# Attention's values products in float32, even and odd key tiles in two halves of the array's columns

## The chip, the cores and the metric

One core of a Trainium2 chip runs the whole program. TensorE (PE, with its weight loads as PEld) multiplies into PSUM; VectorE (DVE), ScalarE (ACT) and GpSimd (POOL) do the rest, and SyncE's queue (SP) issues the transfers. The metric is the device time of one execution in microseconds; a kernel is timed by the median of its runs.

## What is computed

Three layers follow each other. The first is attention with a mask: each query and key is assigned to the nearest of 16 centroids, and a query sees only the keys of its own cluster. Batch 2, 8 heads, 768 tokens, 64 numbers a head. The two layers behind it (a token and channel mixer, and one with cosine and sine) are not touched by the change.

```python
scores = scale * np.matmul(q, k.transpose(0, 1, 3, 2))
scores = np.where(mask, scores, -1000000000.0)
scores = scores - np.max(scores, axis=-1, keepdims=True)
attn = np.exp(scores)
attn = attn / (np.sum(attn, axis=-1, keepdims=True) + 1e-09)
return np.matmul(attn, v).astype(np.float32)
```

## The kernel before

Products are made near float32 accuracy out of a rounded format, float32r, which the array takes in one trip: an operand x is split into h = round(x) and l = x - h, and the products of the parts are summed in PSUM. A split costs one rounding copy and one subtraction (`split_sb`, `split_ps`).

The attention stage goes through 48 units in order. A unit is 256 queries (two tiles of 128) of one head; a head has three units, a pair of heads six, and there are eight pairs. With n for the loop's turn, PE gets `scores(n)`, `turn(n-1)` and `values(n-2)` (`SKEW = 2`), and a scheduler puts the instructions of each engine in their final order: one that stands later in the program can come earlier if it is ready.

- `scores` (line 381): for each of two query tiles four products of 384 columns into a PSUM tile of two banks (two such tiles), DVE's negated maximum over 768 columns (`nm`, line 401), ACT's exponential into `e` (line 403).
- `turn` (line 410): the numerators `e` are turned so that keys lie in partitions, three PSUM tiles `t` of 512 columns (two key tiles by 256 queries), four turns each (line 418). Each tile is then split into `ph` and `pl`, in float32r. By `KINDS` two of three tiles are of kind A: ACT rounds `ph` out of PSUM and DVE subtracts `pl` (lines 87, 88). The third is of kind C: ACT copies the tile to `raw` (line 424), POOL makes `ph` and `pl` from it (lines 428, 429). The first two units and the last are all of kind A.
- `values` (line 435): the values v are split once a head by POOL into `vs`, with v's rounded part in columns 0 to 63 and its rest in columns 64 to 127 (`load_v`, line 325). Per unit twelve products of 128 stationary columns and 256 moving ones (line 444): six key tiles, each with `ph` and `pl`. Rows 0 to 63 of the result hold the part of the rounded values, rows 64 to 127 that of the rests. ACT copies the lower half to `tmp`, DVE adds the two halves into `xt` (lines 449, 451). There is one PSUM bank for the result.
- `natural` (line 455): once a pair, six turns of `xt` back, and DVE scales by the sums of the numerators.
- `masks` (line 234), once a pair, for the next pair: four float32 products of 32 stationary columns at four places in the array's columns (`sim`, line 244), then DVE's transposition, maximum, comparison `eq` (line 257), second transposition, a counting product `pp` on PE (line 268) and the one-hot rows.
- `split_pair` (line 341), once a pair, on POOL: the split of the next pair's queries and keys. `tok_x` (line 130) splits the tokens of the next layer on POOL, six times behind units 29 to 39 and, there, behind the last raw split (`marks["raw"]`). `load_w` prepares weights of the next layers.

Of the kernel before, what the change touches and what calls it, by code (L numbers as in the profile page):

```python
# [9 lines left out]
F32 = mybir.dt.float32  # L10
F32R = mybir.dt.float32r
BF16 = mybir.dt.bfloat16
U32 = mybir.dt.uint32
AF = mybir.ActivationFunctionType
ALU = mybir.AluOpType
# [3 lines left out]
P = 128  # L19
# [4 lines left out]
C2 = 2.0 * math.pi - 6.28125  # L24
PI_LO = 3.1415925


KINDS = "AACAACAAC"
RAW = 4
HL = 4  # L30

X_AT = (29, 31, 33, 35, 37, 39)
# [10 lines left out]
SKEW = 2  # L43
# [4 lines left out]
def tile_model(ctx: ExitStack, tc: tile.TileContext, qT, kT, v, cent, w1, w2, wc1, wc2, wth, wri, wch, out):  # L48


    nc = tc.nc
    B, H, D, S = qT.shape
    NT = S // P
# [12 lines left out]
    marks = {}  # L66
# [8 lines left out]
    def split_sb(h, l, x, rnd, sub):  # L75

        if rnd == "p":
            nc.gpsimd.tensor_scalar(out=h, in0=x, scalar1=1.0, scalar2=0.0, op0=ALU.mult, op1=ALU.add)
        elif rnd == "v":
            nc.vector.tensor_copy(out=h, in_=x)  # L80
        else:
            marks["h"] = nc.scalar.activation(out=h, in_=x, func=AF.Copy)
        e = nc.gpsimd if sub == "p" else nc.vector
        return e.tensor_tensor(out=l, in0=x, in1=h.bitcast(F32), op=ALU.subtract)

    def split_ps(h, l, ps):
        a = nc.scalar.activation(out=h, in_=ps, func=AF.Copy)  # L87
        return a, nc.vector.tensor_tensor(out=l, in0=ps, in1=h.bitcast(F32), op=ALU.subtract)  # L88
# [41 lines left out]
    def tok_x(b, s, new, by):  # L130

        h, l = (new(f"x{k}{b}{s}") for k in "hl")
        marks["l"] = split_sb(h, l, xn[b * NT + s], *by)
        xs.setdefault(b, []).append((h, l))
# [24 lines left out]
    with ExitStack() as actx:  # L159
        ap = actx.enter_context(tc.tile_pool(name="attn", bufs=1))  # L160
# [39 lines left out]
        for j in range(2):  # L200
            r = slice(64 * j, 64 * j + 64)
# [121 lines left out]
        pairs = {}  # L323

        def load_v(b, h):
            vr = ap.tile([P, NT * D], F32, tag="vr", bufs=2, name=f"vr{b}{h}")
            nc.sync.dma_start(out=vr, in_=v[b, h])
            vs = ap.tile([P, NT, 2 * D], F32R, tag="vs", bufs=2, name=f"vs{b}{h}")
            v3 = vr.rearrange("p (n d) -> p n d", d=D)
            split_sb(vs[:, :, 0:D], vs[:, :, D : 2 * D], v3, "p", "p")  # L330
            return vs

        def load_pair(b, pr):
            ts = []
# [75 lines left out]
        def turn(b, h, u, es):  # L410

            pr = []
            for j in range(NT // 2):
                ps = ps_t.tile([P, 2, 256], F32, tag="t", name=f"t{b}{h}{u}{j}")
                for i in range(2):
                    for a in range(2):
                        kt = 2 * j + a
                        marks["turn"] = nc.tensor.transpose(ps[:, a, i * P : i * P + P], es[i][:, kt * P : kt * P + P], ident)  # L418
                ph = ap.tile([P, 2, 256], F32R, tag="ph", bufs=6, name=f"ph{b}{h}{u}{j}")
                pl = ap.tile([P, 2, 256], F32R, tag="pl", bufs=6, name=f"pl{b}{h}{u}{j}")  # L420
                kind = "A" if (b, h, u) in (units[0], units[1], units[-1]) else KINDS[3 * u + j]
                if kind in "BC":
                    raw = ap.tile([P, 2, 256], F32, tag="pr", bufs=2, name=f"pr{b}{h}{u}{j}")
                    nc.scalar.activation(out=raw, in_=ps, func=AF.Copy)  # L424
                    if kind == "B":
                        nc.scalar.activation(out=ph, in_=ps, func=AF.Copy)
                    else:
                        nc.gpsimd.tensor_scalar(out=ph, in0=raw, **one)  # L428
                    marks["raw"] = nc.gpsimd.tensor_tensor(out=pl, in0=raw, in1=ph.bitcast(F32), op=ALU.subtract)  # L429
                else:  # L430
                    marks["ph"], marks["pl"] = split_ps(ph, pl, ps)
                pr.append((ph, pl))
            return pr

        def values(b, h, u, pr, vs):

            if (b, h, u) == units[-1]:
                ps = ps_s.tile([P, 2, 512], F32, tag="s", name="olast")[:, 0, :]
            else:
                ps = ps_o.tile([P, 512], F32, tag="o", name=f"o{b}{h}{u}")  # L440
            order = range(NT)
            for n, kt in enumerate(order):
                for k, p in enumerate(pr[kt // 2]):
                    nc.tensor.matmul(  # L444
                        ps[:, :256], vs[:, kt, :], p[:, kt % 2, :],
                        start=n == 0 and k == 0, stop=n == NT - 1 and k == 1,
                    )
            tmp = ap.tile([64, 256], F32, tag="tmp", bufs=2, name=f"tmp{b}{h}{u}")
            marks["tmp"] = nc.scalar.activation(out=tmp, in_=ps[64:128, :256], func=AF.Copy)
            r0 = 64 * (h % 2)  # L450
            nc.vector.tensor_tensor(  # L451
                out=xts[b, h // 2][r0 : r0 + 64, u * 256 : u * 256 + 256], in0=ps[0:64, :256], in1=tmp, op=ALU.add
            )

        def natural(b, pr):

# [28 lines left out]
        gen = iter(())  # L485
        units = [(b, h, u) for b, h in heads for u in range(NT // 2)]
        es, prs = {}, {}
        late = []
        for n in range(len(units) + SKEW):
            if n < len(units):  # L490
                b, h, u = units[n]
                if u == 0 and h % 2 == 0:
                    sums[b, h // 2] = small.tile([P, NT, 2], F32, tag="sm", bufs=2, name=f"sm{b}{h}")
                    xts[b, h // 2] = ap.tile([P, S], F32, tag="xt", bufs=2, name=f"xt{b}{h}")
                if n != 1:
                    es[n] = scores(b, h, u, ops[b, h])
                if n == 0:
                    next(first, None)
                    place(1, ms[0, 0])
                    scored = marks["scores"]  # L500
                    es[1] = scores(*units[1], ops[b, h])
                    with tc.issue_after(marks["max"].ins):
                        ops[heads[1]] = prep_first(*heads[1])
                    marks["scores"] = scored
                    for w, k in zip(WARM[1:], ("cps", "sim", "scores")):
                        with tc.issue_after(marks[k].ins):
                            warm_up(w)
                h1 = n // 3 + 1
                if 1 < h1 < len(heads) and u == PREP[h1 % 2]:
                    b2, h2 = heads[h1]  # L510
                    ops[b2, h2] = prep(b2, h2, ms[b2, h2 // 2])
                p1 = n // 6 + 1
                if p1 < len(heads) // 2:
                    pr = heads[2 * p1][0], heads[2 * p1][1] // 2
                    if n % 6 == PAIR_AT[0]:
                        raws = load_pair(*pr)
                    if n % 6 == PAIR_AT[1]:
                        split_pair(*pr, raws)
                    if n % 6 == PAIR_AT[2]:
                        gen = masks(*pr)  # L520
            if n >= 3:
                for _ in range(PACE):
                    next(gen, None)
            if n == 42:
                mctx.close()
            if 0 <= n - 1 < len(units):
                prs[n - 1] = turn(*units[n - 1], es.pop(n - 1))
            if n < 3:
                with tc.issue_after((marks["turn"] if n else marks["scores"]).ins):
                    for _ in range(PACE):  # L530
                        next(gen, None)
            if 0 <= n - SKEW:
                b, h, u = units[n - SKEW]
                values(b, h, u, prs.pop(n - SKEW), ops[b, h][4])
                if h % 2 == 1 and u == NT // 2 - 1:
                    late.append((n + 1, b, h // 2))
            while late and (n >= late[0][0] or n == len(units) + SKEW - 1):
                _, b, pr = late.pop(0)
                natural(b, pr)
            if n in X_AT:  # L540
                with tc.issue_after(marks["raw"].ins):
                    tok_x(0, X_AT.index(n), part, "pp")
            if n in W1_AT:
                with tc.issue_after(marks["exp"].ins):
                    i = len(w1s)
                    w1s.append(load_w(w1[:, i * 512 : i * 512 + 512], f"w1_{i}", W1_AT[n]))
            if n == len(units):
                with tc.issue_after(marks["tmp"].ins), tc.issue_after(marks["ph"].ins), tc.issue_after(marks["pl"].ins):
                    for i in range(NT // 2):
                        w2s.append(load_w(w2[:, :, i * 256 : i * 256 + 256], f"w2_{i}", "pv"))  # L550

# [252 lines left out]
```

## Time and profile before

| | us |
|---|---|
| median of 3 runs | 685.1 (683.76 to 690.17) |
| the profiled execution | 684.49 |
| its span | 682.8 |
| busy PE, PEld, DVE, ACT, POOL | 649.9, 553.9, 437.0, 367.4, 367.2 |
| mean granted TensorE clock | 0.987 of full speed |

The span is the profiled part of one execution. A busy PE is not a PE at its peak: matmuls are pipelined and their ends are modelled, so the time that a matmul holds the array is read from one start to the next. The chain of waits follows the work that ended last backwards; its PE pieces run from start to start. A group's line gives the count, the busy time, the mean of one in ns, and the engine's idle time ahead of it with what ended it. PEclk 1.0 is 2.4 GHz, 0.5 is 1.2 GHz.

### The profile page before, as it was taken

To read this page: it belongs to the slowest core of one execution; us is meant where nothing else is said; L and a number is where in the kernel's file an instruction comes from. 1 tells how busy PE (TensorE), PEld (TensorE's weight loads), DVE (VectorE), ACT (ScalarE), POOL (GpSimd) and SP (SyncE) were. 2 spreads that over 40 slices of the span, in tenths; PEclk is the share of its full clock that TensorE was granted. 3 is DMA by queue.
4 is the path that set the end of the run, shared out by engine and by line. 5 is a ranking of instruction groups with operands and counts; after the bars stand their busy time and mean duration, and the time that the engine had idled before them with its cause. 6 is when DMAs were issued, how large, how long until landed. Compare 5 with 4: busy or idle time off the path is not lost.

```text
span 682.8 us, 10123 instructions
## 1 busy us (share of the span) xinstructions
PE 649.9 (95%) x3591; PEld 553.9 (81%) x3591; DVE 437.0 (64%) x700; ACT 367.4 (54%) x701; POOL 367.2 (54%) x353
## 2 busy tenths in 40 slices
PE   7899999989979998999999999999999999999997
PEld 5788897988869786888888878888887878888886
DVE  5988989898897985657665434446668784422112
ACT  6687887877857883336543530327578683320000
POOL 8285957759786853116886630512458787532000
PEclk9999999999989999999999999999999999999999
DMA  8554745445451312002443420220021424310001
GB/s 289 160 137 102 176 108 142 110 118 117 94 120 46 86 55 94 32 31 94 143 135 125 139 77 31 63 62 0 1 63 61 124 64 137 81 59 32 15 32 46
DMA packets 24209, 61.43 MB, mean 90 GB/s; under 512 B 4256, under 2 KB 7520, under 8 KB 24160
## 3 DMA queue, kind: packets, MB, share of 16 engines
q1 hardware_dynamic: 24160, 60.80, 31.4%
q8 instruction: 28, 0.46, 0.3%
q14 instruction: 21, 0.17, 0.1%
HBM read 39.65 MB, written 3.15 MB: 63 GB/s over the span
## 4 chain that ended last, share of the span: by engine, by line
PE 79%; ACT 8%; DVE 6%; issue 3%; POOL 2%; DMA 2%; ACTq 0%; POOLq 0%; DVEq 0%
PE o L444 8%; PE t L418 8%; PE c L125 5%; PE c L126 5%; PE c L124 5%; PE r L124 5%; PE r L126 4%; PE r L125 4%; PE s L398 4%; PE y L126 4%; PE y L125 4%; PE y L124 4%; PE s L399 4%; ACT e L403 2%; ACT ph L87 2%
## 5 line engine op out<-in xcount | busy, mean ns | idle before, releaser
L401 DVE TENSOR_REDUCE nm<-s 128x1 f32<-128x768 f32 x96 | 90.7, 951 | 19.2 <-PE s L399 18.7
L403 ACT ACTIVATE e<-s,nm 128x768 f32<-128x768 f32 x96 | 86.9, 906 | 22.6 <-DVE nm L401 21.3
L418 PE MATMUL t<-ident,e 128*128 128x128 f32 x576 | 80.5, 277 | 5.7 <-DVE pl L88 4.7
L398 PE MATMUL s<-k,qh 128*128 128x384 f32 x188 | 70.3, 374 | 10.4 <-ACT e L403 10.4
L418 PEld LDWEIGHTS t<-ident,e 128*128 128x128 f32 x576 | 66.6, 141 | 14.9 <-DVE pl L88 7.1
L444 PE MATMUL o<-ph,vs 128*128 128x256 f32 x282 | 74.1, 295 | 2.3 <-DVE xt L451 1.9
L444 PE MATMUL o<-pl,vs 128*128 128x256 f32 x282 | 71.7, 287 | 0.0
L88 DVE TENSOR_TENSOR pl<-t,ph 128x512 fp32r<-128x512 f32 x99 | 65.0, 675 | 3.3 <-ACT ph L87 2.1
L399 PE MATMUL s<-k,q 128*128 128x384 f32 x192 | 65.4, 344 | 1.3 <-ACT k L274 1.3
L87 ACT ACTIVATE ph<-t 128x512 fp32r<-128x512 f32 x99 | 55.6, 597 | 14.3 <-PE t L418 10.1
L429 POOL TENSOR_TENSOR pl<-pr,ph 128x512 fp32r<-128x512 f32 x45 | 58.9, 1309 | 1.6
L428 POOL TENSOR_SCALAR ph<-pr 128x512 fp32r<-128x512 f32 x45 | 28.3, 628 | 55.7 <-ACT pr L424 49.7
L444 PEld LDWEIGHTS o<-ph,vs 128*128 128x128 f32 x282 | 54.4, 193 | 4.0 <-DVE xt L451 3.2
L124 PE MATMUL r<-ul,c_h 128*128 128x512 f32 x144 | 56.5, 396 | 0.4 <-DVE ul L88 0.4
L126 PE MATMUL y<-zh,k_h 128*128 128x512 f32 x144 | 56.8, 394 | 0.0
L125 PE MATMUL y<-zh,k_l 128*128 128x512 f32 x144 | 56.8, 394 | 0.0
L125 PE MATMUL c<-c_h,rl 128*128 128x512 f32 x144 | 56.0, 390 | 0.7 <-DVE rl L645 0.7
L124 PE MATMUL y<-zl,k_h 128*128 128x512 f32 x144 | 56.7, 394 | 0.0
L114 POOL TENSOR_TENSOR c_f<-c_f,c_raw 128x512 uint32<-128x512 uint32 x24 | 31.6, 1316 | 45.7 <-issue 28.0
L125 PE MATMUL r<-uh,c_l 128*128 128x512 f32 x144 | 56.1, 390 | 0.0
L126 PE MATMUL r<-uh,c_h 128*128 128x512 f32 x144 | 56.0, 390 | 0.0
L126 PE MATMUL c<-c_h,rh 128*128 128x512 f32 x144 | 56.0, 390 | 0.0
(201 smaller groups left out, 1607.7 us busy)
## 6 DMA issues: line engine op xcount, KB each, us to landing
c_raw<-wc SPq DMA_DIRECT2D x24, 512.0 KB, 3.3
k_raw<-wri SPq DMA_DIRECT2D x18, 512.0 KB, 3.6
qh<-qh SPq DMA_DIRECT2D x28, 192.0 KB, 3.0
k<-kh SPq DMA_DIRECT2D x28, 192.0 KB, 4.0
ql<-qT SPq DMA_DIRECT2D x8, 384.0 KB, 3.1
kl<-kT SPq DMA_DIRECT2D x8, 384.0 KB, 3.8
vr<-v SPq DMA_DIRECT2D x16, 192.0 KB, 2.6
w_raw<-w SPq DMA_DIRECT2D x6, 512.0 KB, 3.9
```

Source lines behind the costliest of these rows:

```text
L87: a = nc.scalar.activation(out=h, in_=ps, func=AF.Copy)
L88: return a, nc.vector.tensor_tensor(out=l, in0=ps, in1=h.bitcast(F32), op=ALU.subtract)
L124: nc.tensor.matmul(ps, ah, bl, start=first and i == 0, stop=False)
L125: nc.tensor.matmul(ps, al, bh, start=False, stop=False)
L126: nc.tensor.matmul(ps, ah, bh, start=False, stop=last and i == n - 1)
L398: nc.tensor.matmul(ps[:, half, :NH], qh[:, c], k1[:, n], start=True, stop=False)
L399: marks["scores"] = nc.tensor.matmul(ps[:, half, :NH], ql[:, c], kk[:, n], start=False, stop=True)
L401: marks["max"] = nc.vector.tensor_reduce(out=nm, in_=ps[:, :, :NH], axis=AX.XY, op=ALU.max, negate=True)
L403: marks["exp"] = nc.scalar.activation(out=e.rearrange("p (a n) -> p a n", a=2), in_=ps[:, :, :NH], func=AF.Exp, bias=nm, accum_out=sums[b, ...
L418: marks["turn"] = nc.tensor.transpose(ps[:, a, i * P : i * P + P], es[i][:, kt * P : kt * P + P], ident)
L429: marks["raw"] = nc.gpsimd.tensor_tensor(out=pl, in0=raw, in1=ph.bitcast(F32), op=ALU.subtract)
L444: nc.tensor.matmul(ps[:, :256], vs[:, kt, :], p[:, kt % 2, :], start=n == 0 and k == 0, stop=n == NT - 1 and k == 1,)
```

## The change

`load_v` loads v as it is, in float32, into three buffers `vs`; POOL's split of v is gone, and `vr`. `turn` copies each of the three tiles `t` once, in float32, into `p` (twelve buffers): the first two by ACT, the third by DVE; the splits into `ph` and `pl` and the raw copies are gone. `values` makes six float32 products a unit: 64 stationary columns, 256 moving ones. Even key tiles go to columns 0 to 63 of the array and rows 0 to 63 of the result, odd ones to columns 64 to 127 and rows 64 to 127; `tmp` and the sum of the two halves stay as they are. `values` may start on PE only behind the last turn that was issued (`issue_after(marks["turn"])`); `GROUP = 1` makes a group of one unit. The first token splits no longer stand behind a raw split, and the last weight loads stand behind `pA` and `pV`.

```diff
-KINDS = "AACAACAAC"
+KINDS = "AAV"
+GROUP = 1
+PB = 12
         def load_v(b, h):
-            vr = ap.tile([P, NT * D], F32, tag="vr", bufs=2, name=f"vr{b}{h}")
-            nc.sync.dma_start(out=vr, in_=v[b, h])
-            vs = ap.tile([P, NT, 2 * D], F32R, tag="vs", bufs=2, name=f"vs{b}{h}")
-            v3 = vr.rearrange("p (n d) -> p n d", d=D)
-            split_sb(vs[:, :, 0:D], vs[:, :, D : 2 * D], v3, "p", "p")
-            return vs
+            vs = ap.tile([P, NT * D], F32, tag="vs", bufs=3, name=f"vs{b}{h}")
+            nc.sync.dma_start(out=vs, in_=v[b, h])
+            return vs.rearrange("p (n d) -> p n d", d=D)
...
-                ph = ap.tile([P, 2, 256], F32R, tag="ph", bufs=6, name=f"ph{b}{h}{u}{j}")
-                pl = ap.tile([P, 2, 256], F32R, tag="pl", bufs=6, name=f"pl{b}{h}{u}{j}")
...
-                    marks["ph"], marks["pl"] = split_ps(ph, pl, ps)
-                pr.append((ph, pl))
+                p = ap.tile([P, 2, 256], F32, tag="p", bufs=PB, name=f"p{b}{h}{u}{j}")
+                if KINDS[j] == "A":
+                    marks["pA"] = nc.scalar.activation(out=p, in_=ps, func=AF.Copy)
+                else:
+                    marks["pV"] = nc.vector.tensor_copy(out=p, in_=ps)
+                pr.append(p)
...
-            for n, kt in enumerate(order):
-                for k, p in enumerate(pr[kt // 2]):
+            for i, (n, pr, vs) in enumerate(us):
+                po = ps[:, 256 * i : 256 * i + 256]
+                for kt in range(NT):
+                    r = 64 * (kt % 2)
                     nc.tensor.matmul(
-                        ps[:, :256], vs[:, kt, :], p[:, kt % 2, :],
-                        start=n == 0 and k == 0, stop=n == NT - 1 and k == 1,
+                        po[r : r + 64, :], vs[:, kt, :], pr[kt // 2][:, kt % 2, :], start=kt < 2, stop=kt >= NT - 2,
+                        tile_position=(0, r),
                     )
...
-                values(b, h, u, prs.pop(n - SKEW), ops[b, h][4])
+                group.append((n - SKEW, prs.pop(n - SKEW), ops[b, h][4]))
+                if len(group) == GROUP:
+                    with tc.issue_after(marks["turn"].ins):
+                        values(group)
+                    group = []
...
             if n in X_AT:
-                with tc.issue_after(marks["raw"].ins):
-                    tok_x(0, X_AT.index(n), part, "pp")
+                tok_x(0, X_AT.index(n), part, "pp")
...
-                with tc.issue_after(marks["tmp"].ins), tc.issue_after(marks["ph"].ins), tc.issue_after(marks["pl"].ins):
+                with tc.issue_after(marks["tmp"].ins), tc.issue_after(marks["pA"].ins), tc.issue_after(marks["pV"].ins):
```

## Rows read from the trace of the kernel before

**Rows 1.** The page: the span, and the chain that ended last by engine.

```profile
span 682.8 us, 10123 instructions
...
PE 79%; ACT 8%; DVE 6%; issue 3%; POOL 2%; DMA 2%; ACTq 0%; POOLq 0%; DVEq 0%
```

**Rows 2.** Windows: stretch, its length, busy us of PE, PEld, DVE, ACT, POOL; clock.

```profile
48.00:78.00 30.00, 28.01 (x210) 25.78 (x209) 26.29 (x46) 23.40 (x50) 21.56 (x23) 1.00 0.52 122
...
195.00:225.00 30.00, 25.09 (x169) 23.52 (x167) 25.80 (x38) 19.25 (x41) 19.34 (x20) 0.89 0.39 88
```

**Rows 3.** The chain of waits, 62 to 105 us: start, length, engine, tile, line.

```profile
62.09 1.44 PE o L444 x12
...
64.23 1.31 PE t L418 x12
...
65.54 0.18 PE s L398
...
69.68 1.07 PE o L444 x9
...
71.46 0.35 PE o L444 x3
...
75.60 0.78 PE sim L244 x8
...
85.30 1.00 ACT e L403 x2
...
104.66 0.78 PE sim L244 x8
```

**Rows 4.** Tile eq (duration min/median/max), then the timeline around 195 us.

```profile
L257 DVE TENSOR_TENSOR eq<-sT,mx x8: 534/1304/4924, 9.5 to 195.0; 128x384 bf16<-128x384 f32 x8
...
195.00 4.92 DVE L257 TENSOR_TENSOR eq<-sT,mx 128x384 bf16<-128x384 f32 x1
...
198.90 0.62 POOL L428 TENSOR_SCALAR ph<-pr 128x512 fp32r<-128x512 f32 x1
...
201.45 1.11 PE L418 MATMUL t<-ident,e 128*128 128x128 f32 x4 [3.55 <-DVE pl L88]
```

**Rows 5.** Timeline around two sim products: start, length, engine, line, tiles, shapes.

```profile
45.07 0.52 PE L244 MATMUL sim<-ql,cst 128*32 128x384 f32 x2
...
45.42 0.49 PE L244 MATMUL sim<-ql,cst 128*32 128x384 f32 x2
...
45.85 0.44 PE L398 MATMUL s<-k,qh 128*128 128x384 f32 x1
...
46.13 0.34 PE L399 MATMUL s<-k,q 128*128 128x384 f32 x1
...
192.56 0.34 PE L399 MATMUL s<-k,q 128*128 128x384 f32 x1
...
192.82 0.52 PE L244 MATMUL sim<-ql,cst 128*32 128x384 f32 x2
...
192.82 0.11 PEld L244 LDWEIGHTS sim<-ql,cst 128*32 128x32 f32 x2 [0.25 <-issue]
...
192.85 0.12 PEld L244 LDWEIGHTS sim<-ql,cst 128*32 128x32 f32 x2
```

**Rows 6.** Groups, 17 to 262 us: shapes, count, busy us, mean ns, idle before.

```profile
L88 DVE TENSOR_TENSOR pl<-t,ph 128x512 fp32r<-128x512 f32 x99 | 65.0, 675 | 3.3 <-ACT ph L87 2.1 <-PE o L444 0.4
...
L87 ACT ACTIVATE ph<-t 128x512 fp32r<-128x512 f32 x99 | 55.6, 597 | 14.3 <-PE t L418 10.1 <-PE o L444 3.5
...
L424 ACT ACTIVATE pr<-t 128x512 f32<-128x512 f32 x45 | 27.1, 603 | 6.7 <-PE t L418 6.4 <-POOL kl L84 0.2
...
L428 POOL TENSOR_SCALAR ph<-pr 128x512 fp32r<-128x512 f32 x45 | 28.3, 628 | 55.7 <-ACT pr L424 49.7 <-PE o L444 5.9
...
L429 POOL TENSOR_TENSOR pl<-pr,ph 128x512 fp32r<-128x512 f32 x45 | 58.9, 1309 | 1.6
...
L250 DVE STREAM_TRANSPOSE sT<-sim 128x384 f32<-128x384 f32 x7 | 4.0, 573 | 0.1
```

More of the change, by code (lines that the diff above doesn't have):

```diff
@@ L418, in turn @@
                         marks["turn"] = nc.tensor.transpose(ps[:, a, i * P : i * P + P], es[i][:, kt * P : kt * P + P], ident)
-                ph = ap.tile([P, 2, 256], F32R, tag="ph", bufs=6, name=f"ph{b}{h}{u}{j}")
-                pl = ap.tile([P, 2, 256], F32R, tag="pl", bufs=6, name=f"pl{b}{h}{u}{j}")
[L421 to L429, printed above, removed]
-                else:
-                    marks["ph"], marks["pl"] = split_ps(ph, pl, ps)
@@ L432, in turn, with values @@
-                pr.append((ph, pl))
-            return pr
-        def values(b, h, u, pr, vs):
-            if (b, h, u) == units[-1]:
+                p = ap.tile([P, 2, 256], F32, tag="p", bufs=PB, name=f"p{b}{h}{u}{j}")
+                if KINDS[j] == "A":
+                    marks["pA"] = nc.scalar.activation(out=p, in_=ps, func=AF.Copy)
+                else:
+                    marks["pV"] = nc.vector.tensor_copy(out=p, in_=ps)
+                pr.append(p)
+            return pr
+        def values(us):
+            if us[-1][0] == len(units) - 1:
@@ L438, in values @@
                 ps = ps_s.tile([P, 2, 512], F32, tag="s", name="olast")[:, 0, :]
             else:
-                ps = ps_o.tile([P, 512], F32, tag="o", name=f"o{b}{h}{u}")
-            order = range(NT)
-            for n, kt in enumerate(order):
-                for k, p in enumerate(pr[kt // 2]):
+                ps = ps_o.tile([P, 512], F32, tag="o", name=f"o{us[0][0]}")
+            outs = []
+            for i, (n, pr, vs) in enumerate(us):
+                po = ps[:, 256 * i : 256 * i + 256]
+                for kt in range(NT):
+                    r = 64 * (kt % 2)
@@ L444, in values @@
                     nc.tensor.matmul(
-                        ps[:, :256], vs[:, kt, :], p[:, kt % 2, :],
-                        start=n == 0 and k == 0, stop=n == NT - 1 and k == 1,
-                    )
[L448 to L453, printed above, removed]
+                        po[r : r + 64, :], vs[:, kt, :], pr[kt // 2][:, kt % 2, :], start=kt < 2, stop=kt >= NT - 2,
@@ new lines, in values @@
+                        tile_position=(0, r),
+                    )
+                outs.append((units[n], po))
+            for (b, h, u), po in outs:
+                tmp = ap.tile([64, 256], F32, tag="tmp", bufs=2, name=f"tmp{b}{h}{u}")
+                marks["tmp"] = nc.scalar.activation(out=tmp, in_=po[64:128, :], func=AF.Copy)
+                r0 = 64 * (h % 2)
+                nc.vector.tensor_tensor(
+                    out=xts[b, h // 2][r0 : r0 + 64, u * 256 : u * 256 + 256], in0=po[0:64, :], in1=tmp, op=ALU.add
+                )
@@ L487, in tile_model @@
         es, prs = {}, {}
-        late = []
+        late, group = [], []
         for n in range(len(units) + SKEW):
```

## Prediction, before the change was run

> **What bounds the kernel now.** I read the page first [rows 1]: 682.8 us of span, and PE is 79% of the chain that ended last. That share is a mean over stages, so I went on to the one stage that the change touches: attention, from the first turned tile at 17 us to about 256. In its windows [rows 2] DVE is busy 26.3 of 30 us and PE 28.0, by modelled ends. The chain of waits [rows 3] tells more, since its PE pieces run from start to start. One unit (256 queries of a head) takes 1.44 for twelve values products, 1.31 for twelve turns and 8 x 0.175 = 1.40 for scores: 4.15 us. A pair of heads is six units, 24.9, and has one cluster product (sim, 0.78), one count product (384 columns, as a score: 0.17) and six turns of its output (6 x 0.109): 26.5 us of PE work. Sim starts at 75.60 and again at 104.66. So a cycle is 29.06 us and PE idles 2.6 of it. The idle is not spread: up to sim the chain is PE alone, after it the chain goes through ACT's exponentials [rows 3]. In that part DVE makes the next pair's masks.
>
> Over the stage: 48 x 4.15 + 8 x 1.6, less 1.7 for the last values products, which run behind it, = 210 of 239 us. About 30 us of PE idle is all that a lighter DVE, ACT or POOL can give back. The rest is PE work.
>
> One piece of it stands out [rows 4]. The mask comparison eq (line 257) takes 0.53 us at its shortest, 1.3 in the middle and 4.92 once. That one ends at 199.92, 0.4 us after a POOL instruction that began at 198.90 and took 0.62: eq reads two SBUF tiles and waits for a gap in POOL. The Trainium skill has such a rule (SBUF — State Buffer, section "Who interferes with whom"): a DVE instruction with two SBUF inputs contends with a GpSimd one that reads SBUF, and the later one blocks. By that rule whatever stays on POOL can still hold eq, and this case would then keep some of its 7 us. Behind eq stand the reduction, the exponential and the turn: PE waits 3.55 us [rows 4], and the mean granted clock from 195 to 225 is 0.89 [rows 2], which is 0.11 x 2 x 30 = 6.6 us at 1.2 GHz. I price the event at 3.55 of waiting and 3.3 lost to half clock, 7 us.
>
> **The change, part by part.** *Values on PE.* Removed: 1.44 us a unit. Added: six float32 products, each with 64 stationary columns, even key tiles in array columns 0 to 63, odd ones in 64 to 127. The nearest rows are sim's [rows 5]: four float32 products side by side, 32 stationary columns and 384 moving ones, two records each. The first records start at 45.07, the second ones at 45.42. So the parts of the array do run together, and a record holds its part for 0.33 to 0.35 us: 384 columns twice at 2.4 GHz (0.32) and a little. For 256 columns that is 0.215 to 0.235. A half has three products, six records, in a row: 1.29 to 1.41. Then the way in and out. In: from 192.56 to 192.82, where a score alone takes 0.175: 0.09. Out: from 45.42 to 45.85 is 0.43, less the record's 0.33: 0.10; and the next product starts 0.28 after that one instead of 0.175: 0.10. Together 0.29 a visit. Values then cost 1.58 to 1.70 a unit; I take 1.61, near the low end, because sim as a whole (0.78 with its way out) fits it. 48 x (1.61 - 1.44) = +8 us, bounds +7 and +12.
>
> *More visits.* In a cycle, some units' twelve products are cut into 9 and 3 [rows 3], two of the six. That costs nothing today; after the change each piece is a visit of its own. Values are now placed behind the last turn, which forbids a cut by turns, but not one by scores. Two cuts in eight cycles are 16 extra visits at 0.29: 0 to +5, I take +2.
>
> *Evacuations* [rows 6]. Removed, over the three tiles of a unit: ACT's ph, DVE's pl (675 ns), ACT's raw copy, POOL's ph and pl (628 and 1309 ns). Added: two ACT copies and one DVE copy a unit. ACT's price is that of its raw copy, 603 ns. A DVE copy of 512 columns out of PSUM has no row; below by DVE's 384-column transposition out of PSUM (573), above by L88 (675), which reads the same tile and another. I take 0.65, by L88. DVE: 99 x 0.675 - 48 x 0.65 = 36 us less in the stage, some 4.2 a cycle. ACT: 99 x 0.597 + 45 x 0.603 - 96 x 0.603 = 28 less. POOL: 45 x 1.94 = 87 less, and the split of the values.
>
> *What that gives back.* Nothing while PE is the chain. In the two units of a cycle in which the masks are made, DVE sheds 2 x 0.7 = 1.4 us, and eq up to 1.3 - 0.53 = 0.8: 1.4 to 2.2 against 2.6 of idle. I take 1.8. Seven cycles: 12. Of the event at 195, POOL's list loses its raw splits, but the splits of keys and tokens stay, so eq can still wait; I take 5 of the 7 us. After 225 the idle is mostly the last head's own path: 1 of 5. Together -18. Bounds: -8 (the event and a little) and -26 (all but 4).
>
> *At nothing:* v is loaded straight into vs with a third buffer (the same 16 issues on SP's queue, and no wait for vr); twelve p buffers for six of each part, the same bytes. The first token splits no longer wait for a raw split: POOL, 87 us lighter, hides them; without that cover they would lie beside eq, as in the event at 195, where I left 2 us. The last weight loads follow pA and pV instead of ph and pl, evacuations of the same unit.
>
> **Sum.** The profiled execution took 684.5 us, 1.7 more than its span. 684.5 + 8 + 2 - 18 = 676.5. The median of the three runs, 685.1, is 0.6 above that execution: 677. Ends: 684.5 + 7 - 26 = 665.5 and 684.5 + 12 + 5 - 8 = 693.5.
>
> **Rivals.** (1) *The idle stays* (0.15). The PE work grows for certain; the wait may not shrink, since DVE keeps four reductions and every mask step in those two units. For it: the chain's last link there is the exponential behind a reduction [rows 3], neither of which is touched. Against: the lo splits stand between the reductions on DVE. With 6 given back instead of 18: 689.
>
> (2) *Side by side, but a record late* (0.08). If products had to start in program order, the second record of one half would hold back the first of the other, and six steps become seven: 48 x 0.22 = 11 us more, 688. Sim's first records start together although each has its second to come [rows 5], which speaks against it; but sim loads no third set of weights into the same columns. The Trainium skill has that order (TensorE: Matmul & The Clock Gate, Part 3, "What overlaps and what doesn't": matmuls strictly first in, first out); sim's rows are hard to fit to it.
>
> (3) *Slower: the split array becomes the bound* (0.12). If the halves run one after the other, twelve steps of 0.215 and a visit of 0.29 are 2.87 us a unit: 48 x 1.43 = 69 us on PE, and with 26 of the idle gone 684.5 + 69 - 26 = 727. In a milder form of the same, weight loads of 0.11 us [rows 5] lie bare before each of the six steps: 48 x 0.66 = 32 us, less 18: 698. It cancels the gain from 0.37 us a unit on (18/48), and is slower by over 1% from 0.52 on. Against it: sim's loads for the second records (192.85) start while the first records run (192.82). The same section of the skill lets a load overlap a running matmul only where their row groups differ, and both halves here take all 128 rows; sim's loads disagree with it.
>
> (4) *Nearly all idle goes* (0.10). DVE falls to about 22 us a cycle and ACT to 20, so PE could run throughout as it does up to sim: 667.
>
> **Chances.** The forecast has 0.55; its own range is 669 to 684. About 1% (6.9 us) is what a measurement of this kernel can tell from no change. Faster, below 678.2: two thirds of the forecast (0.37) and (4): 0.47. Slower, above 692: (3) and 0.03 for the ends of (1) and (2): 0.15. Within: the rest, 0.38. The range, 666 to 692, reaches from (4) to just past (1) and (2) and leaves out (3) and a little below.
>
> **What would show it.** Right: values records of the two halves starting a few ns apart, 0.21 to 0.24 from one record of a half to its next; 1.6 us from a unit's first to the next full-array product; cycles of 28 to 28.5 us; eq at 0.5 to 1.2; clock 1.0 from 195 to 225; past 300 us nothing but a shift. Wrong: the halves 0.2 us apart (2, 3); cycles still of 29 with PE waiting for exponentials (1); many more than 60 visits. Half clock while the array is split would break the sum; sim's rows give no sign of it.

## Result and profile after

The changed kernel takes 665.0 us (median of 4 runs, 663.11 to 666.67), the kernel before on the same chip 687.6 (683.76 to 691.18): a ratio of 0.967 with a 95% interval of 0.960 to 0.974. That is faster, as forecast (677), and 1 us under the low end of the range (666). The profiled execution took 664.99, its span is 663.3: 19.5 less than before [rows 1], where the sum had 8.

The page of the changed kernel: span, busy time by engine, and the chain that ended last by engine.

```profile
span 663.3 us, 9795 instructions
...
PE 646.8 (98%) x3591; PEld 517.7 (78%) x3591; DVE 401.2 (60%) x649; ACT 344.9 (52%) x653; POOL 257.6 (39%) x231
...
PE 86%; ACT 4%; DVE 3%; POOL 3%; issue 2%; DMA 2%; SPq 0%; POOLq 0%; ACTq 0%
```

DVE lost 36 us and POOL 110 against the table of before; PE's share of the chain rose from 79 to 86%. Windows of the changed kernel (columns as in [rows 2]), one cycle and the stretch of the event:

```profile
75.00:103.00 28.00, 28.00 (x212) 21.62 (x211) 21.71 (x39) 20.05 (x42) 6.86 (x6) 1.00 0.59 136
...
195.00:225.00 30.00, 29.47 (x216) 23.42 (x215) 23.47 (x46) 23.27 (x50) 6.39 (x6) 1.00 0.41 98
```

PE has work throughout both stretches, and the granted clock from 195 to 225 us is 1.00 where it was 0.89 [rows 2]. The chain of waits of the changed kernel, around two cluster products and at the last of them:

```profile
73.03 0.78 PE sim L246 x8
...
76.68 1.45 PE o L438 x12
78.13 0.59 PE t L417 x4
...
100.74 0.78 PE sim L246 x8
...
185.35 0.78 PE sim L246 x8
```

From sim to sim it is 27.71 us here; 27.7 and 28.5 alternate, 28.16 on average over five. Before, [rows 3] show a cycle of 29.06; the five up to the last sim average 29.55 (45.07 to 192.82 [rows 5]). The last sim came at 192.82 before [rows 5] and comes at 185.35: 7.5 us are saved up to there. The rest is behind it. The last unit's products, first of before (its products with `ph`, then with `pl`), then of the changed kernel (weight loads left out; duration min/median/max, first and last start):

```profile
L444 PE MATMUL olast<-ph,vs x6: 283/283/284, 255.9 to 260.9; 128*128 128x256 f32 x6
L444 PE MATMUL olast<-pl,vs x6: 283/283/283, 259.8 to 261.0; 128*128 128x256 f32 x6
```

```profile
L438 PE MATMUL olast<-p,vs x12: 379/379/430, 239.2 to 242.6; 128*64 128x256 f32 x12
```

From the last sim to the last values product it was about 68 us and is 57: 11 us saved in the stage's tail alone. The two layers behind it take about what they took (663.3 - 242.6 = 420.7, and 682.8 - 261.0 = 421.8).

### The profile page after: what moved, and what is told of

Read it like the earlier page. It is cut to its first block, busy times and chain, and to the rows that moved or that the text cites. A ratio compares the mean times of both kernels' runs of the same rounds, so it can differ in the third digit from the quotient of the medians.

```text
span 663.3 us, 9795 instructions
## 1 busy us (share of the span) xinstructions
PE 646.8 (98%) x3591; PEld 517.7 (78%) x3591; DVE 401.2 (60%) x649; ACT 344.9 (52%) x653; POOL 257.6 (39%) x231
## 4 chain that ended last, share of the span: by engine, by line
PE 86%; ACT 4%; DVE 3%; POOL 3%; issue 2%; DMA 2%; SPq 0%; POOLq 0%; ACTq 0%
PE o L438 10%; PE t L417 9%; PE s L397 5%; PE r L126 5%; PE r L127 5%; PE r L128 5%; PE c L126 5%; PE c L127 5%; PE c L128 5%; PE s L398 5%; PE y L128 4%; PE y L127 4%; PE y L126 4%; PE po L126 2%; PE po L128 2%
## 5 line engine op out<-in xcount | busy, mean ns | idle before, releaser
L402 ACT ACTIVATE e<-s,nm 128x768 f32<-128x768 f32 x96 | 86.7, 905 | 29.4 <-DVE nm L400 28.1
L397 PE MATMUL s<-k,qh 128*128 128x384 f32 x188 | 71.9, 382 | 2.5 <-ACT e L402 2.3
L438 PE MATMUL o<-p,vs 128*64 128x256 f32 x564 | 71.2, 388 | 0.0
L420 ACT ACTIVATE p<-t 128x512 f32<-128x512 f32 x96 | 52.2, 594 | 25.4 <-PE t L417 25.0
L126 PE MATMUL c<-c_l,rh 128*128 128x512 f32 x144 | 55.2, 391 | 0.0
L438 PEld LDWEIGHTS o<-p,vs 128*64 128x64 f32 x564 | 36.3, 136 | 22.7 <-issue 5.9
L80 POOL TENSOR_SCALAR qh<-ql 128x768 fp32r<-128x768 f32 x7 | 5.8, 835 | 100.9 <-DMA qh<-qh 100.8
L397 PEld LDWEIGHTS s<-k,qh 128*128 128x128 f32 x188 | 35.4, 188 | 11.1 <-ACT e L402 5.6
L398 PEld LDWEIGHTS s<-k,q 128*128 128x128 f32 x192 | 36.7, 192 | 3.8 <-ACT k L276 3.4
```

The source lines that it names most:

```text
L126: nc.tensor.matmul(ps, ah, bl, start=first and i == 0, stop=False)
L397: nc.tensor.matmul(ps[:, half, :NH], qh[:, c], k1[:, n], start=True, stop=False)
L398: marks["scores"] = nc.tensor.matmul(ps[:, half, :NH], ql[:, c], kk[:, n], start=False, stop=True)
L402: marks["exp"] = nc.scalar.activation(out=e.rearrange("p (a n) -> p a n", a=2), in_=ps[:, :, :NH], func=AF.Exp, bias=nm, accum_out=sums[b, ...
L420: marks["pA"] = nc.scalar.activation(out=p, in_=ps, func=AF.Copy)
L438: nc.tensor.matmul(po[r : r + 64, :], vs[:, kt, :], pr[kt // 2][:, kt % 2, :], start=kt < 2, stop=kt >= NT - 2, tile_position=(0, r),)
```

## Experiments

Each time is the median of its runs beside the kernel before on the same chip, where that took 684.3 to 689.4; a ratio is to that. The theory by then: PE's price is about as forecast, and DVE's lighter load gives the idle time back. The rivals: the order of the values on PE does it; or it is what the products wait for, and not how much the engines do.

**The change in two halves.** *e1* takes the change's evacuations alone, and so leaves out the numerators' remainders: each rounded copy is read twice. The change's twelve buffers come with it: at three tiles a unit they are four units deep, where six were two.

```diff
-                ph = ap.tile([P, 2, 256], F32R, tag="ph", bufs=6, name=f"ph{b}{h}{u}{j}")
...
+                ph = ap.tile([P, 2, 256], F32R, tag="ph", bufs=12, name=f"ph{b}{h}{u}{j}")
+                if j < 2:
+                    marks["ph"] = nc.scalar.activation(out=ph, in_=ps, func=AF.Copy)
                 else:
-                    marks["ph"], marks["pl"] = split_ps(ph, pl, ps)
-                pr.append((ph, pl))
+                    marks["pl"] = nc.vector.tensor_copy(out=ph, in_=ps)
+                marks["raw"] = marks["ph"]
+                pr.append((ph, ph))
```

> The kernel before with the evacuations of the change alone: every turned tile is copied once, rounded to float32r (two by ACT, the third by DVE), twelve buffers; PE keeps its twelve products of 128 stationary columns, the second of each pair reading the same rounded copy. The part of the result that comes from the numerators' remainders is left out. Theory (light evacuations free PE of its waits, the split array costs PE some 0.10 us a unit): PE work as before and waits as after, so 665 - 5 = 658 to 662. Rival (the gain comes from placing values behind the last turn): no such placing here, so 676 or more. Rival (the float32 products themselves are cheaper than they look): 668 to 676.

Measured: 653.8, ratio 0.948 [0.943, 0.953]. Its chain of waits:

```profile
69.75 0.78 PE sim L244 x8
...
76.86 1.44 PE o L437 x12
...
96.43 0.78 PE sim L244 x8
```

A cycle is 26.68 us, five times running: the 26.5 of PE work, and nothing else. All the idle time goes when the evacuations are lighter: 32.4 us of span (650.4). The changed kernel, which has the split array besides, is slower than this by 10.7 us (664.5 in *a0* below): that is the price of the split array with the waits that come with it.

*e2* is the other half: the new products (on the rounded numerators and the values as loaded, so that the numerators' remainders have no part in the output), with all old evacuations still made.

```diff
-            vr = ap.tile([P, NT * D], F32, tag="vr", bufs=2, name=f"vr{b}{h}")
+            vr = ap.tile([P, NT * D], F32, tag="vr", bufs=3, name=f"vr{b}{h}")
...
-            return vs
+            return v3
...
+            for kt in range(NT):
+                r = 64 * (kt % 2)
+                nc.tensor.matmul(
+                    ps[r : r + 64, :256], vs[:, kt, :], pr[kt // 2][0][:, kt % 2, :].bitcast(F32), start=kt < 2, stop=kt >= NT - 2,
+                    tile_position=(0, r),
+                )
...
-                values(b, h, u, prs.pop(n - SKEW), ops[b, h][4])
+                with tc.issue_after(marks["turn"].ins):
+                    values(b, h, u, prs.pop(n - SKEW), ops[b, h][4])
```

> The kernel before with the products of the change alone: six float32 products by halves of the columns, placed behind the last turn, reading the rounded part of the numerators and v as loaded; ACT, DVE and POOL still make both parts of the numerators and of v as before. The remainders are made and not used. Theory: PE's price is paid (48 x 0.10 = 5 us, a little more if a unit's products are cut) and no wait goes: 688 to 695, 3 to 8 above the kernel before. Rival (placing or products bring the gain): 670 to 678.

Measured: 677.1, ratio 0.981 [0.977, 0.985]. PE does some 9 to 11 us more (48 x 0.18, worked out below, or e1's 10.7), DVE, ACT and POOL do all that they did, and the kernel is 12 us faster. So some 21 to 23 us come back without any of the load gone. That contradicts the theory. What is gone here is that products read `pl` and the split values, and the old order.

**The order.** *e8* gives before the change's order, *e7* takes it from the changed kernel; *a0* is the changed kernel once more, on their chip.

```diff
-                values(b, h, u, prs.pop(n - SKEW), ops[b, h][4])
+                with tc.issue_after(marks["turn"].ins):
+                    values(b, h, u, prs.pop(n - SKEW), ops[b, h][4])
```

> The kernel before with one edit: the twelve products of a unit may start on PE only behind the last turn issued, as in the change; evacuations, splits and products are those of before. e2 gave back 12 us with all the old evacuations left in, so either the placing or the products did it. If the placing did it: 670 to 677 beside a kernel before of 685 to 689. If it is nothing by itself: 683 to 690.

> The changed kernel without the placing of the values behind the last turn. If the light evacuations alone take the waits away (as e1 has it, which ran without the placing): 662 to 668, with a few more visits to the split array at about 0.3 us each. If the placing carries a part of the gain: 672 to 680.

> The changed kernel as it is, for a time on the same chip as its variants: 663 to 668.

Measured: e8 688.8, ratio 1.001 [0.998, 1.004]; e7 667.0, 0.968 [0.964, 0.973]; a0 664.5, 0.965 [0.960, 0.970]. The placing brings before nothing. In the changed kernel it keeps the visits at 49 pieces for 48 units, 59 without it; the intervals of e7 and a0 overlap, but all four runs of e7 are above all four of a0, by 2.5 us in the median.

**The load put back.** To the changed kernel come instructions that the change removed, with outputs that nothing reads: *e4* one DVE subtraction a unit, *e3* POOL's rounding and remainder of the third tile, *e11* an ACT copy and the DVE subtraction, *e9* all of these. POOL's split of the values stays out of e9: POOL is busy for 344.6 us there, for 367.2 before. The diff of e9 (the others are parts of it):

```diff
                 pr.append(p)
+                if j == 1:
+                    d2 = ap.tile([P, 2, 256], F32R, tag="dv", bufs=1, name=f"dv{b}{h}{u}{j}")
+                    nc.vector.tensor_tensor(out=d2, in0=ps, in1=p, op=ALU.subtract)
+                if j == 2 and (b, h, u) not in (units[0], units[1], units[-1]):
+                    d0, d1, d3 = (ap.tile([P, 2, 256], F32R, tag=f"dp{k}", bufs=1, name=f"dp{k}{b}{h}{u}") for k in range(3))
+                    nc.scalar.activation(out=d3, in_=ps, func=AF.Copy)
+                    nc.gpsimd.tensor_scalar(out=d0, in0=p, **one)
+                    nc.gpsimd.tensor_tensor(out=d1, in0=p, in1=d0.bitcast(F32), op=ALU.subtract)
```

> The changed kernel, and DVE subtracts once a unit a copied tile from its PSUM tile into a tile that nobody reads (48 x 0.675 = 32 us of DVE, about what the change takes off it). If DVE's load made PE wait: 674 to 682, with PE waiting for exponentials again. If POOL's load was it: 665 to 669. Both rise: each has its part.

> The changed kernel, and POOL makes a rounded part and a remainder of each unit's third tile that nobody reads (45 tiles, 1.94 us each, 87 us of POOL, as before the change); the order on PE is that of the changed kernel. If POOL's load was what made PE wait (eq held by POOL, and the clock that fell behind it): eq up to 1.2 to 4.9 us again and the time 672 to 680. If DVE's own load was it: eq up by some 0.6 us a pair, 665 to 669.

> The changed kernel with ACT's and DVE's former work back (a copy and a subtraction a unit that nobody reads), not POOL's. With POOL's as well it took 676, 12 more than the changed kernel; DVE's alone cost about 1. If ACT's copy is the load that matters: 671 to 676. If it takes POOL beside DVE (eq held again): 664 to 668.

> The changed kernel with all the work back that the change takes off the three engines, as work whose results nobody reads: once a unit a subtraction on DVE, a copy on ACT (45 of 48 units), a rounding and a subtraction on POOL (45 of 48). e3 and e4 put back POOL's and DVE's alone and cost 4 and about 0. If the waits came of the sum of the loads: 676 to 685. If they came of the way the old parts hung together (ph, then pl, then the product; raw, then POOL, then the product): 667 to 673.

Measured: e4 665.7, ratio 0.964 [0.960, 0.968]; e3 668.9, 0.968 [0.964, 0.973]; e11 672.5, 0.984 [0.978, 0.990]; e9 676.2, 0.983 [0.977, 0.988]. One DVE instruction a unit costs nothing that can be measured, POOL's two some 3 to 4 us, ACT's and DVE's together 8 by the medians and 13 by the ratios, and all of it 12 (676.2 against 664.5, same chip). The windows of e9:

```profile
75.00:103.00 28.00, 27.44 (x205) 21.24 (x205) 24.32 (x44) 23.28 (x48) 15.76 (x17) 1.00 0.54 128
```

ACT and DVE are back at the load of before (DVE 24.3 of 28 us, before 26.3 of 30), yet PE waits for little, and a cycle is mostly 28.7. So this load explains about 12 of some 30 us of idle time that went.

**Who reads the remainders.** Here every evacuation of before is made; only what the products read differs, and the remainders that are not read have no part in the output. *e10* reads no `pl`, *e12* not POOL's, *e13* not DVE's.

```diff
-                pr.append((ph, pl))
+                pr.append((ph, ph))
```

```diff
-                pr.append((ph, pl))
+                pr.append((ph, ph if kind == "C" else pl))
```

```diff
-                pr.append((ph, pl))
+                pr.append((ph, pl if kind == "C" else ph))
```

> The kernel before with one edit: of each pair of products the second reads ph too. DVE and POOL still make every pl, but nothing reads it, so a unit's products wait for ph alone; the part of the result that comes from the remainders is left out. All loads, all PE work and the placing are those of before. e2 (old loads, new products, nothing reads pl) was 12 us faster than before. If the wait for pl at the end of the chain turn, ph, pl is what e2 took away: 670 to 678, and faster than e2 by the price of the split array or not by much slower. If it was the new products themselves: 685 to 690.

> The kernel before; of the tiles of the third kind (raw copy, POOL's rounding, POOL's remainder) the second product reads ph, so no product waits for POOL's pl; DVE's pl is read as before. With no pl read at all it took 668.5 beside 684 to 689. If POOL's chain (a raw copy of 0.6, then 1.94 us of POOL in its queue) is what was late: 668 to 673. If DVE's: 682 to 689. Shared: 674 to 681.

> The kernel before; of the tiles of the first kind (ACT rounds, DVE subtracts) the second product reads ph, so no product waits for DVE's pl; POOL's is read as before. The counterpart of e12: if POOL's chain was late, 682 to 689; if DVE's, 668 to 673; shared, 674 to 681.

Measured: e10 668.5, ratio 0.977 [0.972, 0.983]; e12 666.6, 0.973 [0.966, 0.980]; e13 689.0, 1.004 [1.001, 1.008]. Products that don't read POOL's remainder make the kernel 21 us faster with all the work in place; not reading DVE's, of which there are twice as many (99 and 45 [rows 6]), gives nothing. The windows of e12, and its tile eq:

```profile
75.00:103.00 28.00, 27.21 (x208) 25.23 (x207) 25.94 (x46) 23.12 (x50) 20.79 (x23) 1.00 0.57 138
```

```profile
L257 DVE TENSOR_TENSOR eq<-sT,mx x8: 641/1144/1700, 9.7 to 192.6; 128x384 bf16<-128x384 f32 x8
```

DVE is as busy as before, 25.9 of 28, and eq is still long in its median (1.14); only the one of 4.92 is gone. Tile eq of e13, where that one is back:

```profile
L257 DVE TENSOR_TENSOR eq<-sT,mx x8: 534/1199/4920, 9.4 to 200.1; 128x384 bf16<-128x384 f32 x8
```

What PE and ACT wait for tells the two kinds apart. From the list of waits in the attention stage (engine, tile, line, releaser: us in all, times, longest), of before, e13 and e12 in turn:

```profile
ACT e L403 <- DVE nm L401: 21.3, 20, 3.7
...
PE s L398 <- ACT e L403: 9.8, 15, 1.1
```

```profile
ACT e L403 <- DVE nm L401: 24.8, 23, 3.9
...
PE s L398 <- ACT e L403: 11.4, 15, 1.0
...
ACT ph L87 <- PE o L444: 5.1, 2, 3.5
...
POOL ph L428 <- PE o L444: 3.2, 4, 1.2
```

```profile
ACT e L403 <- DVE nm L401: 11.6, 19, 1.8
...
PE s L398 <- ACT e L403: 2.7, 3, 1.4
```

The line of PE is the one to go by: ACT's own idle is no price, and the changed kernel has 28.1 us of it. No values product waits long for `pl` itself: the time shows as scores that wait for exponentials, which wait for maxima. It is the same wait that the forecast took for DVE's load, and it goes with DVE's load unchanged.

Not all of e12's gain lies there. The last sim and the last values product, of before (its last product stands with the result) and of e12:

```profile
L244 PE MATMUL sim<-ql,cst x32: 482/486/511, 5.8 to 193.2; 128*32 128x384 f32 x32
```

```profile
L244 PE MATMUL sim<-ql,cst x32: 482/486/510, 5.9 to 189.6; 128*32 128x384 f32 x32
L444 PE MATMUL olast<-pl,vs x6: 278/283/364, 246.7 to 248.1; 128*128 128x256 f32 x6
```

Of 17.9 us of span (682.8 - 664.9), 3.6 are saved up to the last sim, 9.3 in the stage's tail, and 5.0 in the two layers behind the stage, which the edit doesn't touch (the granted clock is 0.96 from 261.1 to 300 us before, and 1.00 in e12 from 248.1 to 287).

How the reading of POOL's remainder reaches those places, these runs don't tell. Three ways are open. The late remainder may hold the chain itself. With another reader the scheduler also made another order for PE and DVE (68 values pieces in place of 71), which may place everything so that DVE comes late. Or it is the buffers: before, ACT's and POOL's `ph` wait 3.5 and 5.9 us for a values product to free one of the six [rows 6], in e13 5.1 and 3.2, in e12 and in the changed kernel never. A version of before with more buffers for `ph` and `pl`, or the changed kernel with six, would bear on the third; neither was run.

*e17* comes at it from the other side: all tiles are of kind A, so that POOL is out of the chain and DVE makes every remainder; nothing is left out.

```diff
-KINDS = "AACAACAAC"
+KINDS = "AAAAAAAAA"
...
-                with tc.issue_after(marks["raw"].ins):
+                with tc.issue_after(marks["pl"].ins):
```

> The kernel before with all three tiles of a unit split by ACT and DVE: no raw copy, no POOL in the chain from turn to product; every product reads what it read. DVE gets 45 subtractions more (30 us), ACT 45 copies fewer in pairs (one instead of one: as before), POOL 87 us less. If the late link was POOL's chain and DVE's room suffices: 668 to 678. If DVE then becomes the bound (its stage share goes from 88% to about 98%): 684 to 700.

Measured: 679.6, ratio 0.986 [0.977, 0.995]. DVE gets 45 subtractions more, some 30 us at 675 ns [rows 6], and the kernel is faster by 9.6. If DVE's load alone were the bound, it would be slower. But POOL's load is lighter too (284.4 us busy in place of 367.2), and in the profiled execution the five cycles up to the last sim average 29.6, as before, and no `ph` waits for a buffer. So e17 shows neither that POOL's place in the chain is what makes the cycles long nor that the buffers are.

**The two halves of the array.** *e6* issues a unit's three even key tiles first, then the odd ones. *e5* makes one visit for two units, *e14* the same without the placing.

```diff
-                for kt in range(NT):
+                for kt in (0, 2, 4, 1, 3, 5):
```

```diff
-GROUP = 1
+GROUP = 2
```

```diff
-GROUP = 1
+GROUP = 2
...
-                    with tc.issue_after(marks["turn"].ins):
-                        values(group)
+                    values(group)
```

> The changed kernel with the order of the six products in a unit changed to the three even key tiles and then the three odd ones. If the array lets a product of the free half start past the waiting ones of the other half: 664 to 667, the two halves still a few ns apart. If products start in the order in which they are issued: the second half starts when the first is at its last product, 10 steps instead of 6, 0.86 us a unit, 41 us on PE: 695 to 706.

> The changed kernel with the products of two units in one visit to the split array (the group made two): 24 visits less. If a visit has a fixed price of 0.25 to 0.3 us: 6 to 7 us faster on PE, 658 to 661, unless the products of the first unit, which now come later, make PE wait for other work: then 664 to 670.

> The changed kernel with groups of two units and without the placing behind the last turn. On PE the products then stand in 104 pieces instead of 49. If each piece has its price of way in and out (0.25 to 0.3 us): 664.5 + 55 x 0.28 = 680, 677 to 684. If the price belongs to the products and not to the visit: 662 to 668.

Measured: e6 687.8, ratio 1.005 [1.001, 1.008]; e5 669.6, 0.979 [0.973, 0.984]; e14 680.8, 0.991 [0.988, 0.994]. One unit's twelve records in the timeline (start, length), in the changed kernel with the score ahead of them and the turn behind, and in e6:

```profile
62.63 0.34 PE L398 MATMUL s<-k,q 128*128 128x384 f32 x1
62.90 1.52 PE L438 MATMUL o<-p,vs 128*64 128x256 f32 x12
64.34 0.33 PE L417 MATMUL t<-ident,e 128*128 128x128 f32 x1
```

```profile
101.66 2.00 PE L438 MATMUL o<-p,vs 128*64 128x256 f32 x12
103.59 0.44 PE L397 MATMUL s<-k,qh 128*128 128x384 f32 x1
```

1.52 and 2.00: 0.48 us a unit, 23 us in 48 units, which is all of e6's loss (687.8 - 664.5). The starts in e6 say how. The even half's records start at 101.659, 101.925, 102.141, 102.357, 102.573 and 102.789, the odd half's at 102.147, 102.414, 102.630, 102.845, 103.061 and 103.277. The odd half was free from the beginning and still began two records late, 6 ns behind the first record of the even half's second product: it passed the third even product, which was still waiting, but not the second. Here a product passed one that waited for its half, and not two. In the changed kernel, where even and odd alternate, both halves start 6 to 7 ns apart.

e14's visits are 104 pieces for 48 units, 55 more than a0's, and it takes 16 us more: 0.29 a visit if all of it is the visits (groups of two come with them), which is the price that the prediction had. e5 has 25 pieces, yet loses: a cycle is 28.48 us. What is saved on the array goes elsewhere; where, was not taken apart. Over the stage its scores wait 2.4 us for exponentials, about as in the changed kernel (2.3).

## Why the prediction was right in direction and too high

**Values on PE: right.** Forecast 1.61 us a unit in place of 1.44, +8 us. The halves start 6 to 7 ns apart and a half's records 0.216 apart, as forecast. The rows at e6 show a visit behind a score: 0.27 from the score's start to the first record, where a score alone takes 0.175, so 0.09 for the way in; then 1.44 to the turn. Behind a turn:

```profile
103.41 0.27 PE L417 MATMUL t<-ident,e 128*128 128x128 f32 x1
...
103.62 0.65 PE L438 MATMUL o<-p,vs 128*64 128x256 f32 x4
```

0.20 from the row's last turn to the first record, where a turn alone takes 0.109: again 0.09. The product after the first full-array one is late by 0.055 behind a turn and 0.10 behind a score (0.165 and 0.279 from start to start instead of 0.109 and 0.175). So a unit takes 1.60 to 1.64 us, and PE 48 x 0.18 = 8.6 us more. Only the detail of 1.6 us from a unit's first to the next full-array product was put wrongly: that stretch is 1.45, and the rest lies ahead of it and behind.

**More visits: too high by 2 us.** 16 extra ones were feared, there is at most one (49 pieces for 48 units). Values placed behind the last turn are not cut by scores either. e7 shows what a cut costs: its cycles are 28.13 us, 1.45 more than e1's, which is 6 x 0.18 and 0.37 for the one unit in most cycles that is cut. Both terms together: +10 forecast, 10.7 measured (e1 against a0). Of these 8.6 are the products; the rest goes with waits, such as those of the changed kernel's scores for exponentials:

```profile
PE s L397 <- ACT e L402: 2.3, 4, 0.6
```

Three of the four come before the last sim, where three of five cycles are 28.5 instead of 27.7. So that the sum of the two came out right is in part luck.

**Evacuations: right.** The DVE copy, taken as 0.65 us, took 0.68 in the groups of the changed kernel:

```profile
L422 DVE COPY p<-t 128x512 f32<-128x512 f32 x48 | 32.8, 683 | 1.8 <-PE t L417 1.7
```

**What that gives back: this step failed.** It had 18 of some 30 us. The span fell by 19.5 although PE's work rose by 9: about 28 were given back. By place: up to the last sim 7.5 us and the price of some 35 units on PE (35 x 0.18 = 6.3), 14 where the step had 12; behind it 11 and 13 units' price (2.3), 13 where it had 6 (5 of the event's 7, 1 of the 5 after 225). So up to the last sim the price was nearly right in sum, and most of the error is in the tail, of which nearly all the idle time went.

The reason is in how it priced. It took an idle time that shows behind DVE, counted what DVE sheds beside it, and gave back no more than that. e9 shows the price of the load: with it put back, 12 us are lost. It didn't ask what a product waits for, and it put the twelve buffers at nothing by their bytes, although a unit needs three of them and no longer six. The third tile went from the turn through three instructions more (ACT's raw copy, POOL's `ph`, POOL's `pl`, 603 + 628 + 1309 ns on average [rows 6], without their queues) before its products could run, and the change cuts that to one copy. With the loads in place, products that don't read the remainders gave back 16 (e10) to 21 us (e12), and some 21 to 23 in e2; not reading DVE's alone (e13) gave nothing. e12 has 9.3 us of this in the stage's tail, where the step was most wrong. 12 for the load and 21 for the reading are 33, near the 35.6 by medians of e1, which does both; that the two simply add is not shown. That time goes once the products no longer read POOL's remainder is shown; how that reading reaches DVE's maxima, by its own delay, through the order that the scheduler makes around it or through the buffers, is open, as said at e12.

**The event at 195: right on its cause, too cautious on the rest.** The changed kernel's eq:

```profile
L259 DVE TENSOR_TENSOR eq<-sT,mx x8: 537/549/822, 9.8 to 188.6; 128x384 bf16<-128x384 f32 x8
```

At most 0.82 us, within the forecast's 0.5 to 1.2. The prediction left 2 us for the token splits still on POOL; nothing of it came. With POOL's work back (e3) the longest is 2.46:

```profile
L259 DVE TENSOR_TENSOR eq<-sT,mx x8: 534/674/2465, 9.7 to 191.4; 128x384 bf16<-128x384 f32 x8
```

So POOL does hold eq, by its load, as the prediction said and as the Trainium skill has it (SBUF — State Buffer, "Who interferes with whom"; the traces agree, 2.46 and 4.92 us against 0.53). But e3 as a whole loses 3 to 4 us: by POOL's load alone, holding eq costs no more than that here. And with all of POOL's load in place, e12 has no comparison longer than 1.70: what stands beside it counts too, and not only how much there is.

**The rivals.** (4), nearly all idle goes, 667 with a chance of 0.10, is what came; it deserved more, for the row that spoke for it was there: up to sim, PE ran throughout [rows 3]. (1) fell: cycles are 28.2 and PE's wait for exponentials went from 9.8 to 2.3 us. (2) and (3) fell for this order of the tiles, where the halves start together; e6 shows that (2) is real for another order, and there costs more than its 11 us. The Trainium skill's rule behind it (TensorE: Matmul & The Clock Gate, Part 3, "What overlaps and what doesn't": matmuls strictly first in, first out) is half borne out: one waiting product was passed, two were not.

**What should show.** Cycles of 28 to 28.5 (28.16), eq, the clock of 1.00 from 195 to 225, and only a shift past 300 us came as written; the 1.6 us did not, as said. A cycle as forecast with a time 12 us lower is no contradiction: the tail gave back twice what it was allowed, hardly an extra visit came, and the forecast had started from a cycle of 29.06, where the five of before average 29.55. That cycles of 28 to 28.5 came is thus partly luck: each gave back some 2.5 us (29.55 - 28.16, and 6 x 0.18) where 1.8 was forecast.

## What to carry to other kernels

Before an idle time is priced by the load of the engine that shows behind it, follow one tile from its producer to the product that reads it, and count the units that its buffers hold. Here products that no longer read a slow engine's result gave back 21 us with all the work in place, and putting the work back cost 12; the time had shown as waits elsewhere. A run that keeps all the work and changes only what is read tells load from the rest, though the scheduler's order moves with it. Where two halves of the array run side by side, alternate them in program order.

## What the runs showed of the hardware beyond that

- Products for two halves of the columns, with the same 128 rows, run side by side: a float32 product of 256 columns is two records 0.216 us apart, and the halves' first records start 6 to 7 ns apart.
- In e6 a product whose half was free passed one product waiting for the other half, not two (0.48 us a unit late).
- Going into the split array costs 0.09 us behind a score as behind a turn, and the second full-array product after it is 0.055 to 0.10 late; 55 extra visits in e14 come with 16 us, 0.29 each.
